# Additions, copies and word tiles of a fused attention and MoE kernel moved between ScalarE and VectorE, and matrix products moved ahead of the scores

## The chip, the cores and the metric

The kernel runs on one core of a Trainium2 chip. The time is that of the device in microseconds, from the core's start to its end, and the median of several runs counts. A core has a matrix engine (TensorE, PE in the rows), a vector engine (VectorE, DVE), an engine for functions and copies (ScalarE, ACT), GpSimd (POOL) for plain element work, and SyncE (SP), whose queue issues every DMA of this kernel. Each engine runs its own instructions in the order in which they were written; between engines only semaphores order the work.

## The reference

Four batches of eight heads of windowed attention, with 576 rows of 64 numbers per head, give the rows x (2304 by 512). Then follow two layers without a residual path:

```python
scores = where(mask, q @ k.T / 8, -1e9)             # plain window of 32 (heads 0-3) or dilated by 4 (heads 4-7)
p = exp(scores - max); attn = p / (p.sum(-1) + 1e-9) @ v
x = attn.transpose(0, 2, 1, 3).reshape(2304, 512)
h = x @ w_in                                        # layer one, w_in and w_out are 64-bit floats
x = (h - tanh(h)) @ w_out
logits = x @ phi                                    # layer two: 32 slots, 8 experts
d = softmax over rows; c = softmax over slots
out = c @ concat_e(relu((d.T @ x)_e @ w1[e]) @ w2[e])
```

The epsilon 1e-9 in the denominator of the attention, the copies that bring q and k into place, and the conversion of the 64-bit words of w_in and w_out are what the change touches.

## The kernel before, in words

The rows are taken in five chunks: the first 512 of each batch (chunks 0 to 3), and one last chunk of what is left over of all four. A chunk needs the attention of its batch (values split into a high part `xhi` and a low part `xlo`), and layer one: 16 tiles of h, each of 12 matmuls of 128 by 512 (high by high, low by high, high by low; `emit_h`, L559 to L561), a tanh on ScalarE (L565), a subtraction on VectorE (L568), a transposition on VectorE (L581) and small products with phi (`emit_logits`, L574).

The attention of batch 0 stands alone at the start (0 to about 62 us), written out by a list of due times. The attention of batch 1 is interleaved with layer one of chunk 0, two tiles of h a step in eight steps 0 to 7 (`mixed_step`); batches 2 and 3 are interleaved in the same way with chunks 1 and 2 (`phase_step`). An attention is cut into 12 units. A unit is: scores into one PSUM tile (L349, behind a product that lays down the mask, L331), a maximum over them on VectorE (L359), three or four exponentials with row sums on ScalarE (L362), the epsilon (L371) and a reciprocal (L373) on VectorE, the norm on GpSimd (L374), transposition by TensorE (L383) and a copy of it, and the products with v (L404), whose results go to `xhi` (ScalarE) and `xlo` (VectorE, L440). In batches 0 and 1 q and k are transposed by TensorE (L307) and copied by the engines that the table `ENGS['qk']` names, A for ScalarE and V for VectorE (L102 and L315 or L317).

Chunk 0 also converts the weights. A 64-bit word is turned into a float by a ScalarE instruction on the upper half (`conv_a`, L492) and two VectorE instructions that shift in bits of the lower half (`conv_b`, L500 and L501). For a w_in tile the high part is rounded by a copy (L513, shown under the helper's line L102, engine by `ENGS['wh']`), and the low part is a subtraction on GpSimd (L514). A w_out tile is stored to DRAM, and multiplied with phi at once (`conv_out_c`: transposition L522 and copy; `conv_out_d`: four products L533 and a copy; `conv_out_e`: L546).

The raw words are loaded by SP, two tiles a DMA (L467 w_in, L471 w_out), into places in `gt` that earlier raw words held. A DMA waits until those are read, and the ones behind it in the queue wait with it. A converted w_in tile lies in one place, `b[:, 3]` of `cvb`, until L514 has read it; w_out tiles have four places in `cva`. Of PSUM, the five tiles `mm` go round among all of this.

What each step issues in which order stands in `mixed_step`, L935 to L984.

Of the kernel before, what the change touches and what calls it, by code (L numbers as in the profile page):

```python
# [14 lines left out]
ALU = mybir.AluOpType  # L15
# [20 lines left out]
    ("out", 0): 0, ("out", 2): 1, ("out", 4): 2, ("in", 0): 3, ("in", 2): 0, ("in", 4): 1, ("out", 6): 2, ("in", 6): 3,  # L36
    ("out", 8): 2, ("out", 10): 1, ("in", 8): 2, ("in", 10): 3, ("out", 14): 2, ("in", 14): 3,
}
ENGS = {'qk': 'AAAAVAAVVVAA', 'pt': 'AAA', 'hi': 'AAA', 'rem': 'VVA', 'wh': 'V', 'wt': 'AV', 'wq': 'V', 'wp': 'A'}
WARM = 5  # L40
NWARM = 4
WAT = 0.29
# [21 lines left out]
def moe_kernel(ctx: ExitStack, tc: tile.TileContext, q, k, v, w_in, w_out, phi, w1, w2, out):  # L64
# [258 lines left out]
    def emit_scores(b, i):  # L323
        p, u = PO[i // 3], i % 3
        nb, nq, nk = shape(i)
        ps = mm([128, nb, nk])
        mask = mask_d[:, (0, 4, 2)[u]:(4, 8, 6)[u]] if nb == 4 else mask_p[:, min(u, 1):min(u, 1) + 3]
        by_pe = b < MASKPE
        nr = nq if by_pe else 64
        if by_pe:  # L330
            nc.tensor.matmul(  # L331
                ps.rearrange("p c k -> p (c k)"), lhsT=id2.rearrange("p a k -> p (a k)"),
                rhs=mask[0:64].rearrange("p c k -> p (c k)"), start=True, stop=True,
            )
        for c in range(nb):
            for x in range(2):
                step = 1
                if nb == 4:

                    r2, qi = divmod(2 * u + c // 2, 3)  # L340
                    q0 = 288 * (c % 2) + 144 * r2
                    q0, k0 = q0 + nq * qi, q0 + max(0, nq * qi - 32)
                    if b in VB:
                        q0, k0 = (288 * (c % 2) + r2 + 2 * (t - 288 * (c % 2) - 144 * r2) for t in (q0, k0))
                        step = 2
                else:
                    q0, k0 = nq * (nb * u + c), max(0, nq * (nb * u + c) - 32)
                r = slice(64 * x, 64 * x + 64)
                nc.tensor.matmul(  # L349
                    ps[64 * x:64 * x + nr, c, :], lhsT=qT[b, p][r, q0:q0 + step * (nr - 1) + 1:step],  # L350
                    rhs=kT[b, p][r, k0:k0 + step * (nk - 1) + 1:step],
                    start=not by_pe, stop=True, skip_group_check=True,
                )
        pr = prs.next()[:, 0:nb * nk].rearrange("p (c k) -> p c k", c=nb)
        if not by_pe:
            nc.vector.tensor_tensor(out=pr, in0=ps, in1=mask, op=ALU.add)
            ps = pr
        nm = tiny("nm", 4, 3)[:, 0:nb]
        nc.vector.tensor_reduce(out=nm, in_=ps, op=ALU.max, axis=AX.X, negate=True)  # L359
        sm = tiny("smm", 4, 3)[:, 0:nb]  # L360
        for c in range(nb):
            nc.scalar.activation(  # L362
                out=pr[:, c, :], in_=ps[:, c, :], func=ACTF.Exp, bias=nm[:, c:c + 1],
                accum_out=sm[:, c:c + 1],
            )
        sc_s[b, i] = (pr, sm)

    def emit_norm(b, i):
        nb, nq, nk = shape(i)
        pr, sm = sc_s.pop((b, i))  # L370
        nc.vector.tensor_scalar(out=sm, in0=sm, scalar1=EPS, scalar2=None, op0=ALU.add)  # L371
        rc = tiny("rc", 4, 3)[:, 0:nb]
        nc.vector.reciprocal(out=rc, in_=sm)  # L373
        nc.gpsimd.tensor_tensor(out=pr, in0=pr, in1=rc.unsqueeze(2).to_broadcast([128, nb, nk]), op=ALU.mult)  # L374
        sc_p[b, i] = pr
# [101 lines left out]

    def conv_tiles():
        a, b = unit("cva", [128, 4, 512]), unit("cvb", [128, 4, 512])
        convs["out"], convs["in"] = Ring([a[:, n] for n in range(4)]), Ring([b[:, 3]])  # L480
        convs["wt"] = Ring([b[:, 0].rearrange("p (a b) -> p a b", a=4), b[:, 1].rearrange("p (a b) -> p a b", a=4)])
        convs["wq"] = b[:, 2].rearrange("p (a b) -> p a b", a=4)

# [11 lines left out]
    def conv_b(kind, ft):  # L495
        wl, _ = raw_t.pop((kind, ft))
        f = cvt[kind, ft]
        du = f.bitcast(U32)
        dk = like(f, kind).bitcast(U32)
        nc.vector.tensor_scalar(out=du, in0=du, scalar1=3, scalar2=None, op0=ALU.logical_shift_left)  # L500
        nc.vector.scalar_tensor_tensor(  # L501
            out=dk, in0=wl, scalar=29, in1=dk, op0=ALU.logical_shift_right, op1=ALU.bitwise_or
        )
# [60 lines left out]
    def emit_tanh(ps, g):  # L564
        nc.scalar.activation(out=g, in_=ps, func=ACTF.Tanh)  # L565
# [308 lines left out]
    with tc.manual_schedule():  # L874
# [60 lines left out]
        def mixed_step(an, ch, s, xh, xl, gs, posts):  # L935

            a, b = 2 * s, 2 * s + 1
            if s == 0:
                an.load(3, 2)
            if s < 6:  # L940
                load_w("in", 4 + a)
            if s < 5:
                load_w("out", 6 + a)
            pa, gs[a] = emit_first(ch, xh, xl, a, first), gring.next()
            emit_tanh(pa, gs[a])
            emit_sub(pa, gs[a])
            if s < 7:
                conv_a("in", 2 + a)

            if s:  # L950
                for n in (a - 2, a - 1):
                    emit_gT(ch, n, gs[n])
            an.turn(s)
            if s < 7:
                conv_b("in", 2 + a)
                conv_in_c(2 + a)
            if 0 < s < 6:
                conv_out_c(4 + a)
                conv_out_c(5 + a)
            if s in (2, 4, 6):  # L960
                conv_out_e(3 + a)
            if s < 5:
                conv_a("out", 6 + a)
                conv_a("out", 7 + a)
                conv_b("out", 6 + a)
                conv_b("out", 7 + a)
            if s < 7:
                conv_a("in", 2 + b)
            pb, gs[b] = emit_first(ch, xh, xl, b, first), gring.next()
            emit_tanh(pb, gs[b])  # L970
            an.score(2 * s)
            emit_sub(pb, gs[b])
            an.score(2 * s + 1)
            if s < 7:
                conv_b("in", 2 + b)
                conv_in_c(2 + b)
            an.norms(s)
            an.values(s)
            if 0 < s < 6:
                conv_out_d(4 + a)  # L980
                conv_out_d(5 + a)
            if s:
                emit_logits(ch, a - 1, gs[a - 1])
            emit_logits(ch, a, gs[a])  # L984
# [38 lines left out]
        for ch in range(4):  # L1023
            xh, xl = xhi[ch], xlo[ch]
            if ch == 3:
                late.insert(0, sb.tile([128, 2048], F32, tag="qk", name="ex"))
                xr = unit("xr", [128, 2, KT, 256], F32R)
                nc.scalar.copy(out=xr[:, 0], in_=xrem)
                nc.vector.tensor_tensor(out=xr[:, 1], in0=xrem, in1=xr[:, 0].bitcast(F32), op=ALU.subtract)
                home(0, late)  # L1030
                load_experts()
                gring = Ring(glast)
            else:
                gring = gts
            gs, nxt = {}, None
            for s in range(NFT // 2):
                (phase_step if ch else mixed_step)(an, ch, s, xh, xl, gs, posts)
# [202 lines left out]
```

## Time and profile before

| | |
|---|---|
| median of 3 runs | 473.22 us (471.66 to 473.87) |
| the profiled execution | 473.43 us, of which the span from the first to the last instruction is 471.6 us |
| TensorE busy | 437.3 us, 93% of the span |
| VectorE | 262.3 us, 56% |
| ScalarE | 198.3 us, 42% |
| GpSimd | 77.0 us, 16% |

Matmuls are pipelined, so that TensorE's share is not one of its peak. The shares are means over stages that differ: up to 62 us the attention of batch 0 runs with filler matmuls, from 62 to 157.5 us chunk 0 with the weights' conversion, then three chunks, the rest, and the experts. In the timelines a row is one instruction or several like it: start, duration, engine, line, operation, tile written and tiles read, shapes, count, and in brackets the idle time of the engine before it and what ended that.

### The profile page before, as it was taken

The numbers are of one execution on the slowest core, as the hardware profiler recorded it, in microseconds if no ns is written. First come the engines' busy times: TensorE is split into PE (matmuls) and PEld (weight loads), VectorE is DVE, ScalarE is ACT, GpSimd is POOL, SyncE is SP. The second block draws the span as 40 slices with busy tenths as digits, with TensorE's granted clock in tenths as the row PEclk, the third lists the DMA queues.
The fourth block names the chain that finished last, engine by engine and source line by source line (L and its number), as shares of the span: only waits on it lengthen the run. The fifth ranks groups of instructions, "written<-read, shape, count | busy, mean of one in ns | idle before, by whom it ended". The sixth has DMA issues, their size and how long they took to land.

```text
span 471.6 us, 11459 instructions
## 1 busy us (share of the span) xinstructions
PE 437.3 (93%) x4615; PEld 318.6 (68%) x4615; DVE 262.3 (56%) x631; ACT 198.3 (42%) x683; POOL 77.0 (16%) x95
## 2 busy tenths in 40 slices
PE   6989897998999999999999999999999999999981
PEld 4766566875777685888776778776777689645330
DVE  1555569898887675666575786362744251232141
ACT  3777546664653163564244445422122222213131
POOL 3221313233133331213112031100000000010000
PEclk9999997998999999999999999999999999999996
DMA  8999934966465403162333120248000789899938
GB/s 245 226 238 317 280 146 135 258 179 231 131 169 108 94 1 51 41 89 39 81 67 54 37 41 3 90 182 355 0 1 5 265 318 403 348 375 408 409 131 329
DMA packets 88260, 81.15 MB, mean 172 GB/s; under 512 B 63888, under 2 KB 67728, under 8 KB 88208
## 3 DMA queue, kind: packets, MB, share of 16 engines
q1 hardware_dynamic: 88208, 80.43, 56.0%
q8 instruction: 36, 0.59, 0.5%
q14 instruction: 16, 0.13, 0.1%
HBM read 71.50 MB, written 8.91 MB: 170 GB/s over the span
## 4 chain that ended last, share of the span: by engine, by line
PE 60%; issue 12%; DVE 10%; ACT 7%; DMA 6%; POOL 1%; SPq 1%; ACTq 0%; DVEq 0%; POOLq 0%
PE h L559 11%; PE h L561 10%; PE h L560 10%; PE mm L349 4%; ACT mem L362 4%; PE lg L574 3%; PE h L782 3%; PE mm L404 3%; PE y L807 3%; PE mm L698 3%; PE mm L383 3%; DVE cva L501 2%; DMA raww<-in_moe_w_out_dram 2%; DMA v<-in_v_dram 1%; DMA rqk<-in_k_dram 1%
## 5 line engine op out<-in xcount | busy, mean ns | idle before, releaser
L559 PE MATMUL h<-xhi,wts 128*128 128x512 f32 x256 | 106.6, 416 | 1.1 <-DVE wts L102 0.7
L561 PE MATMUL h<-xhi,wts 128*128 128x512 f32 x256 | 101.3, 396 | 2.0 <-POOL wts L514 2.0
L560 PE MATMUL h<-xlo,wts 128*128 128x512 f32 x256 | 101.2, 395 | 0.0
L565 ACT ACTIVATE mem<-h 128x512 f32<-128x512 f32 x72 | 42.9, 596 | 135.1 <-PE h L561 127.7
L568 DVE TENSOR_TENSOR mem<-h,mem 128x512 f32<-128x512 f32 x72 | 49.4, 686 | 79.8 <-ACT mem L565 79.7
L559 PEld LDWEIGHTS h<-xhi,wts 128*128 128x128 f32 x256 | 49.0, 191 | 17.5 <-issue 5.8
L561 PEld LDWEIGHTS h<-xhi,wts 128*128 128x128 f32 x256 | 48.6, 190 | 14.5 <-POOL wts L514 3.7
L374 POOL TENSOR_TENSOR mem<-mem 128x320 f32<-128x320 f32 (+1 forms) x48 | 33.4, 704 | 148.4 <-DVE mem L373 79.8
L560 PEld LDWEIGHTS h<-xlo,wts 128*128 128x128 f32 x256 | 48.9, 191 | 8.9 <-DVE xlo L440 0.3
L581 DVE STREAM_TRANSPOSE gt<-mem 128x512 f32<-128x512 f32 x64 | 41.1, 684 | 0.0
L362 ACT ACTIVATE mem<-mem 128x80 f32<-128x80 f32 (+1 forms) x84 | 29.7, 355 | 15.6 <-DVE mem L359 15.6
L349 PE MATMUL mm<-qk 64*64 64x96 f32 (+2 forms) x672 | 34.2, 245 | 1.9 <-ACT qk L315 1.7
L362 ACT ACTIVATE mem<-mm,mem 128x80 f32<-128x80 f32 (+1 forms) x84 | 26.9, 338 | 17.4 <-DVE mem L359 17.2
L349 PEld LDWEIGHTS mm<-qk 64*64 64x64 f32 (+1 forms) x672 | 27.5, 132 | 8.6 <-ACT qk L315 3.3
L514 POOL TENSOR_TENSOR wts<-cvb,wts 128x512 fp32r<-128x512 f32 x16 | 20.6, 1289 | 73.6 <-DVE wts L102 34.9
L102 ACT COPY mem<-mm 96x384 f32<-96x384 f32 (+4 forms) x64 | 26.3, 439 | 8.6 <-PE mm L383 6.9
L383 PE MATMUL mm<-mem 112*80 112x112 f32 (+1 forms) x168 | 23.9, 276 | 5.0 <-ACT cvb L492 2.7
L574 PE MATMUL lg<-mem 128*32 128x128 f32 x576 | 25.9, 279 | 0.9 <-DVE mem L568 0.9
L404 PE MATMUL mm<-mem,v 80*64 80x48 f32 (+1 forms) x672 | 26.0, 226 | 0.5 <-ACT mem L102 0.5
L404 PEld LDWEIGHTS mm<-mem,v 80*64 80x64 f32 (+1 forms) x672 | 22.1, 137 | 5.4 <-issue 2.2
L383 PEld LDWEIGHTS mm<-mem 112*80 112x80 f32 (+1 forms) x168 | 16.7, 125 | 9.5 <-POOL mem L374 4.4
L574 PEld LDWEIGHTS lg<-mem 128*32 128x32 f32 x576 | 15.3, 109 | 11.3 <-issue 9.0
(170 smaller groups left out, 643.4 us busy)
## 6 DMA issues: line engine op xcount, KB each, us to landing
ex<-in_moe_w_dram SPq DMA_DIRECT2D x21, 1024.0 KB, 10.7
gt<-in_moe_w_out_dram SPq DMA_DIRECT2D x7, 1024.0 KB, 8.1
gt<-in_moe_w_in_dram SPq DMA_DIRECT2D x7, 1024.0 KB, 7.8
gt<-in_moe_w_dram SPq DMA_DIRECT2D x6, 1024.0 KB, 11.5
mem<-in_moe_w_dram SPq DMA_DIRECT2D x5, 1024.0 KB, 8.3
wo_dram<-cva SPq DMA_DIRECT2D x16, 256.0 KB, 6.2
wo<-wo_dram SPq DMA_DIRECT2D x4, 1024.0 KB, 7.9
out_dram<-o SPq DMA_DIRECT2D x8, 512.0 KB, 4.8
```

The source lines that it names most:

```text
L349: nc.tensor.matmul(ps[64 * x:64 * x + nr, c, :], lhsT=qT[b, p][r, q0:q0 + step * (nr - 1) + 1:step], rhs=kT[b, p][r, k0:k0 + step * (nk - ...
L362: nc.scalar.activation(out=pr[:, c, :], in_=ps[:, c, :], func=ACTF.Exp, bias=nm[:, c:c + 1], accum_out=sm[:, c:c + 1],)
L374: nc.gpsimd.tensor_tensor(out=pr, in0=pr, in1=rc.unsqueeze(2).to_broadcast([128, nb, nk]), op=ALU.mult)
L383: nc.tensor.transpose(ps[:, c, :], pr[0:P, c, :], ident[0:P, 0:P])
L404: nc.tensor.matmul(o[64 * hh:64 * hh + 64, col:col + nq], lhsT=vt[b, p](n, hh), rhs=pt[:, c, 64 * x:64 * x + nq], start=True, stop=True,)
L559: nc.tensor.matmul(ps, lhsT=wh, rhs=xh[:, kt, :], start=(n == 0), stop=False)
L560: nc.tensor.matmul(ps, lhsT=wh, rhs=xl[:, kt, :], start=False, stop=False)
L561: nc.tensor.matmul(ps, lhsT=wl, rhs=xh[:, kt, :], start=False, stop=(n == KT - 1))
L565: nc.scalar.activation(out=g, in_=ps, func=ACTF.Tanh)
L568: nc.vector.tensor_tensor(out=g, in0=ps, in1=g, op=ALU.subtract)
L574: nc.tensor.matmul(lgs[ch][32 * j:32 * j + 32, 0:128], lhsT=wp[:, ft, :], rhs=g[:, 128 * j:128 * j + 128], start=(ft == 0), stop=(ft == NF ...
L581: nc.vector.transpose(out=gt[:, ft, :], in_=g)
```

## The change

Six edits, of which the first reaches all four batches:

- The epsilon is added by a ScalarE instruction right behind a unit's exponentials (L366 in the changed kernel), not by VectorE in front of the reciprocal.
- In batch 1 all four copies of q and k of a pair are ScalarE's (two of them were VectorE's).
- The copy that rounds the high part of a w_in tile is ScalarE's for all 16 tiles.
- A converted w_in tile has a second place, `glast[4]`, in a region of `mem` that held g tiles; so chunk 0 has five places for g tiles instead of six, and chunk 1 begins elsewhere in the ring.
- In a step, the conversion of both w_in tiles stands earlier: the even tile's `conv_b` ahead of the transpositions L581, the odd tile's `conv_a` and `conv_b` before the second tile of h; the low part of the odd tile follows the second tanh.
- The products with phi (`conv_out_d`, L533) stand ahead of the scores, not behind the products with v.

```diff
-ENGS = {'qk': 'AAAAVAAVVVAA', 'pt': 'AAA', 'hi': 'AAA', 'rem': 'VVA', 'wh': 'V', 'wt': 'AV', 'wq': 'V', 'wp': 'A'}
+ENGS = {'qk': 'AAAAAAAAVVAA', 'pt': 'AAA', 'hi': 'AAA', 'rem': 'VVA', 'wh': 'A', 'wt': 'AV', 'wq': 'V', 'wp': 'A'}
...
                 accum_out=sm[:, c:c + 1],
             )
+        nc.scalar.activation(out=sm, in_=sm, func=ACTF.Copy, bias=EPS)
         sc_s[b, i] = (pr, sm)

     def emit_norm(b, i):
         nb, nq, nk = shape(i)
         pr, sm = sc_s.pop((b, i))
-        nc.vector.tensor_scalar(out=sm, in0=sm, scalar1=EPS, scalar2=None, op0=ALU.add)
...
-        convs["out"], convs["in"] = Ring([a[:, n] for n in range(4)]), Ring([b[:, 3]])
+        convs["out"], convs["in"] = Ring([a[:, n] for n in range(4)]), Ring([b[:, 3], glast[4]])
...
             if s < 7:
                 conv_a("in", 2 + a)
-
+                conv_b("in", 2 + a)
             if s:
                 for n in (a - 2, a - 1):
                     emit_gT(ch, n, gs[n])
             an.turn(s)
             if s < 7:
-                conv_b("in", 2 + a)
+                conv_a("in", 2 + b)
                 conv_in_c(2 + a)
+                conv_b("in", 2 + b)
...
-            if s < 7:
-                conv_a("in", 2 + b)
             pb, gs[b] = emit_first(ch, xh, xl, b, first), gring.next()
             emit_tanh(pb, gs[b])
+            if s < 7:
+                conv_in_c(2 + b)
+            if 0 < s < 6:
+                conv_out_d(4 + a)
+                conv_out_d(5 + a)
             an.score(2 * s)
             emit_sub(pb, gs[b])
             an.score(2 * s + 1)
-            if s < 7:
-                conv_b("in", 2 + b)
-                conv_in_c(2 + b)
             an.norms(s)
             an.values(s)
-            if 0 < s < 6:
-                conv_out_d(4 + a)
-                conv_out_d(5 + a)
...
-                gring = gts
+                gring = gts if ch else Ring([gts.places[n] for n in (0, 1, 2, 4, 3)])
+                gts.n += 4 * (ch == 1)
```

ScalarE's order in step 0, from the first tanh (L565) to the exponentials (L362), before. Here `cvb` is the even or odd w_in tile, `cva` a w_out tile:

```order
L565 ACTIVATE mem<-h 128x512
L492 ACTIVATE cvb<-gt 128x512
L102 COPY qk<-mm 128x3x2x48
L315 ACTIVATE qk<-mm 128x3x2x48
L492 ACTIVATE cva<-gt 128x512 x2
L492 ACTIVATE cvb<-gt 128x512
L565 ACTIVATE mem<-h 128x512
L362 ACTIVATE mem<-mm,mem 128x80 x8
```

The same stretch of ScalarE now, where L492 and the CAST with `mem` belong to the odd w_in tile in its second place, and L366 is the epsilon:

```order
L565 ACTIVATE mem<-h 128x512
L492 ACTIVATE cvb<-gt 128x512
L102 COPY qk<-mm 128x3x2x48 x2
L315 ACTIVATE qk<-mm 128x3x2x48 x2
L492 ACTIVATE mem<-gt 128x512
L102 CAST wts<-cvb 128x4x128
L492 ACTIVATE cva<-gt 128x512 x2
L565 ACTIVATE mem<-h 128x512
L102 CAST wts<-mem 128x4x128
L362 ACTIVATE mem<-mm,mem 128x80 x4
L366 ACTIVATE mem<-mem 128x4
L362 ACTIVATE mem<-mm,mem 128x80 x4
```

Two copies, two roundings and the two additions have come in, and the odd w_in tile now stands ahead of the two w_out tiles.

VectorE's order in the same step, from the even w_in tile's second instruction (L501 on `cvb`) to the reciprocals (L373), before:

```order
L501 SCALAR_TENSOR_TENSOR cvb<-gt,cvb 128x512
L102 CAST wts<-cvb 128x4x128
L500 TENSOR_SCALAR cva<-cva 128x512
L501 SCALAR_TENSOR_TENSOR cva<-gt,cva 128x512
L500 TENSOR_SCALAR cva<-cva 128x512
L501 SCALAR_TENSOR_TENSOR cva<-gt,cva 128x512
L359 TENSOR_REDUCE mem<-mm 128x4
L568 TENSOR_TENSOR mem<-h,mem 128x512
L359 TENSOR_REDUCE mem<-mm 128x4
L500 TENSOR_SCALAR cvb<-cvb 128x512
L501 SCALAR_TENSOR_TENSOR cvb<-gt,cvb 128x512
L102 CAST wts<-cvb 128x4x128
```

VectorE now, from the same instruction (`mem<-mem` and `mem<-gt,mem` of L500 and L501 are the odd w_in tile):

```order
L501 SCALAR_TENSOR_TENSOR cvb<-gt,cvb 128x512
L500 TENSOR_SCALAR mem<-mem 128x512
L501 SCALAR_TENSOR_TENSOR mem<-gt,mem 128x512
L500 TENSOR_SCALAR cva<-cva 128x512
L501 SCALAR_TENSOR_TENSOR cva<-gt,cva 128x512
L500 TENSOR_SCALAR cva<-cva 128x512
L501 SCALAR_TENSOR_TENSOR cva<-gt,cva 128x512
L359 TENSOR_REDUCE mem<-mm 128x4
L568 TENSOR_TENSOR mem<-h,mem 128x512
L359 TENSOR_REDUCE mem<-mm 128x4
L373 RECIPROCAL mem<-mem 128x4 x2
```

The odd w_in tile has moved from behind the two maxima to ahead of the w_out tiles, and so ahead of the maxima.

TensorE's order at the end of step 1, behind the second tile of h, before:

```order
L561 MATMUL h<-xhi,wts 128x512
L331 LDWEIGHTS mem
L331 MATMUL mm<-mem 128x320
L349 MATMUL mm<-qk 48x80 x8
L331 LDWEIGHTS mem
L331 MATMUL mm<-mem 128x320
L349 MATMUL mm<-qk 48x80 x8
L404 MATMUL mm<-mem,v 64x48 x16
L533 MATMUL mm<-cvb,mem 32x128 x8
L574 MATMUL lg<-mem 32x128 x8
```

The same stretch of TensorE now:

```order
L561 MATMUL h<-xhi,wts 128x512
L533 MATMUL mm<-cvb,mem 32x128 x8
L331 LDWEIGHTS mem
L331 MATMUL mm<-mem 128x320
L349 MATMUL mm<-qk 48x80 x8
L331 LDWEIGHTS mem
L331 MATMUL mm<-mem 128x320
L349 MATMUL mm<-qk 48x80 x8
L404 MATMUL mm<-mem,v 64x48 x16
L574 MATMUL lg<-mem 32x128 x8
```

The products L533 have moved ahead of both scores. The order of SP's DMAs is the same in both kernels.

## Rows read from the trace of the kernel before

**Rows 1.** Busy time in steps 1, 3, 4 of chunk 0; last columns clock, DMA share, GB/s.
```profile
67.12:85.96 18.84, 15.64 (x155) 12.45 (x151) 17.19 (x32) 12.22 (x45) 5.01 (x5) 0.82 0.42 128
...
100.17:114.88 14.71, 12.24 (x141) 9.50 (x137) 11.86 (x29) 8.21 (x29) 3.93 (x4) 0.99 0.74 251
114.88:129.65 14.77, 14.08 (x139) 11.10 (x135) 12.38 (x28) 7.88 (x27) 3.82 (x4) 0.90 0.50 139
```

**Rows 2.** Timeline of TensorE in step 1 and in chunk 1.
```profile
74.84 1.71 PE L383 MATMUL mm<-mem 112*80 112x112 f32 x8 [2.69 <-ACT cvb L492]
...
77.91 0.78 PE L559 MATMUL h<-xhi,wts 128*128 128x512 f32 x1
...
180.07 1.47 PE L698 MATMUL mm<-gt,mem 32*32 32x512 f32 x33 [0.67 <-DVE xlo L440]
```

**Rows 3.** Waits of TensorE from 60 to 165 us: total, times, longest.
```profile
PE mm L533 <- ACT mem L362: 3.2, 3, 2.3
...
PE h L561 <- POOL wts L514: 1.0, 2, 0.6
```

**Rows 4.** Timeline of ScalarE: conversions, copies, and small instructions.
```profile
54.78 0.66 ACT L492 ACTIVATE cvb<-gt 128x512 f32<-128x512 f32 x1 [1.24 <-POOL wts L514]
...
64.18 0.54 ACT L102 COPY qk<-mm 128x288 f32<-128x288 f32 x1
64.55 0.55 ACT L315 ACTIVATE qk<-mm 128x288 f32<-128x288 f32 x1
...
109.50 1.26 ACT L492 ACTIVATE cva<-raww 128x512 f32<-128x512 f32 x2 [3.26 <-DMA raww<-in_moe_w_out_dram]
...
193.40 0.19 ACT L362 ACTIVATION_READ_ACCUMULATOR mem<-mem 128x1 f32 x1
193.49 0.30 ACT L102 CAST xhi<-mm 128x96 fp32r<-128x96 f32 x2
193.69 0.21 ACT L102 COPY mem<-mm 128x64 f32<-128x64 f32 x1
193.79 0.32 ACT L102 CAST xhi<-mm 128x192 fp32r<-128x192 f32 x1
...
246.90 0.28 ACT L639 ACTIVATE mem<-mem 128x1 f32<-128x1 f32 x1
```

**Rows 5.** DMA issues on SP's queue at the start of step 3.
```profile
100.07 0.39 SPq L467 DMA_DIRECT2D gt<-in_moe_w_in_dram  x1
100.56 1.32 SPq L471 DMA_DIRECT2D raww<-in_moe_w_out_dram  x1
```

**Rows 6.** Timeline of VectorE in steps 0 to 2.
```profile
67.13 1.65 DVE L501 SCALAR_TENSOR_TENSOR cva<-gt,cva 128x512 uint32<-128x512 uint32 x1
...
69.76 0.48 DVE L359 TENSOR_REDUCE mem<-mm 128x4 f32<-128x320 f32 x1
...
72.33 0.43 DVE L102 CAST wts<-cvb 128x512 fp32r<-128x512 f32 x1
72.67 0.16 DVE L371 TENSOR_SCALAR mem<-mem 128x4 f32<-128x4 f32 x1
...
73.03 1.09 DVE L371 TENSOR_SCALAR mem<-mem 128x4 f32<-128x4 f32 x1
...
98.86 0.42 DVE L500 TENSOR_SCALAR cvb<-cvb 128x512 uint32<-128x512 uint32 x1
99.31 0.69 DVE L501 SCALAR_TENSOR_TENSOR cvb<-gt,cvb 128x512 uint32<-128x512 uint32 x1
```

**Rows 7.** Timeline of GpSimd in steps 0 and 1.
```profile
66.84 1.39 POOL L514 TENSOR_TENSOR wts<-cvb,wts 128x512 fp32r<-128x512 f32 x1 [8.12 <-DVE wts L102]
...
72.84 1.26 POOL L514 TENSOR_TENSOR wts<-cvb,wts 128x512 fp32r<-128x512 f32 x1 [4.61 <-DVE mem L371]
```

**Rows 8.** Pieces of the chain that ended last, batch 0: start, us, what.
```profile
20.86 0.09 DVE mem L371
...
23.15 1.35 ACT mem L362 x8
```

## The prediction

> **What bounds the kernel now.** I read the engines' shares first (TensorE 93%, so only its idle and slow stretches can be won), then the windows by step, the waits of TensorE, and the timelines around those waits, last the chain and SP's queue. The reader is to see three things.
>
> First, chunk 0 is where TensorE loses time. Step 1 takes 18.84 us and step 4 14.77 with the granted clock at 0.82 and 0.90; step 3 takes 14.71 with TensorE busy for 12.24 of it [rows 1]. [...] In step 3 the second product with phi L533 waits 2.3 us for the exponentials of the step's first scores, whose PSUM tile it takes; three such waits make 3.2 us [rows 3].
>
> Second, what feeds the stall of step 3 is a DMA: ScalarE stood 3.26 us at the w_out words (109.50) with tanh and exponentials queued behind [rows 4]. That DMA was issued at 100.56, right behind the w_in one at 100.07 [rows 5], which waited for the place that the odd w_in tile's L501 of step 2 read last, from 99.31 to 100.00 [rows 6].
>
> Third, VectorE is held by GpSimd. An L501 that takes 0.69 took 1.65 from 67.13, a second L371 1.09 from 73.03 where the one ahead took 0.16 [rows 6]; both end just behind an L514 of GpSimd (66.84 + 1.39, 72.84 + 1.26) [rows 7].
>
> **The change part by part.** The sum is made against the profiled execution, 473.43 us, of which 471.60 are span; that is 0.2 above the median of the runs.
>
> Epsilon on ScalarE, batch 0. No row shows an ACTIVATE of 128x4 that waits for the accumulator read in front of it. Without a wait a small copy costs 0.10 (193.69 to 193.79), which is the low end. [...] High end: 0.19 of read and all 0.28 of the 128x1 ACTIVATE, 0.47 [rows 4]. I take 0.26, nearest to the copy. The chain of batch 0 goes through eleven units' exponentials and from ten of them on through ScalarE's next work (at 23.15, say, eight instructions of 1.35 us that chain on to a copy) [rows 8], so 10 x 0.26 = 2.6 come in. L371 lies on that chain six times, each time 0.26 from the instruction before it to the reciprocal (0.09 of it shown); at one of them the scores behind ScalarE's copies would be later anyway, so 5 x 0.26 = 1.3 go. Net +1.3; with the bounds -0.3 to +3.4.
>
> Second place for a word tile. The odd tile's L492 at 54.78 waited 1.24 for GpSimd [rows 4]. Now it waits for ScalarE's own queue: the even tile's rounding, two copies to xhi and two others, 1.45 us from the end of L501 at 52.94, so it starts at 54.4. Of 1.24 only 0.4 go: -0.4 (0 to -1.2).
>
> Steps 0 and 1. Four copies of q and k stand on ScalarE instead of two. They are 0.37 apart (64.18, 64.55) [rows 4], so the first scores start up to 2 x 0.37 later, and TensorE has nothing else: +0.4 after 0.3 that VectorE's own copies took longer. Behind the copies come the odd L492 (to 66.4), the even rounding (0.66 like the L492, to 67.0), and GpSimd's L514 from 67.0 to 68.3. VectorE does the odd pair from 66.4 to 67.5 (1.1 from 0.42 and 0.69 [rows 6]), is then held to 68.3, does a w_out pair to 69.4, is held again by the odd tile's L514 (69.2 to 70.5), and comes to the first maximum at 71.6, where before it was 69.76 [rows 6]. Then nothing of the conversion is left behind the maxima, so exponentials and norms run through: two times 1.35 and 0.26, reciprocal, norm, and the second transpositions end at about 76.5. Before, they ended at 74.84 + 1.71 [rows 2]. So the stall and its slow clock stay, and this term is +0.4 (-3.5 to +1.5, the ends under the rivals).
>
> [...]
>
> L533 ahead of the scores. Its two tiles now come from copies that were read long before, not from exponentials: -3.2 [rows 3]. The products need the two copies of L522's results; the VectorE one ends about 6 us behind the step's first tanh, when the second tile of h is just done. Cover gone, that is a wait of some tenths. With the idle stretch of step 3 the low clock of step 4 goes: 0.10 of 14.77 lost is 2.95 us at the half level [rows 1], work for 1.5: -1.5. The DMA wait of 3.26 goes too: the odd pair of step 2 is done some 6 us earlier, and so are both DMAs [rows 5]; the place of those words was last read by TensorE in step 1.
>
> Low parts earlier. The h matmuls L561 that waited for L514, 1.0 in two [rows 3]: the later one (0.6) goes, -0.6.
>
> What is late next, steps 2 to 4. VectorE has, from a step's tanh to its first maximum, a subtraction, four pairs of 1.1, two transpositions and three copies, some 7.2 us, and up to two holds by GpSimd of 1.3; then ScalarE two units of exponentials and epsilon, 2.5, and xhi, 0.55. That is 10.2 to 12.8, where TensorE alone needs 12.3 in step 3 (14.71 - 2.34, less some tenths of others) [rows 1]. I take +0.5 for the three steps (0 to +2).
>
> The roundings moved. One is 0.43 on VectorE (72.33) and like an L492, 0.66, on ScalarE [rows 4, 6]; from step 1 on each is covered by the 2.7 us of h behind it, and costs nothing; with that cover gone, 0.66. [...]
>
> Chunks 1 and 2. L698 waits 0.67 for the low parts, which stand behind ScalarE's exponentials, two copies and a tanh (180.07; the same wait in chunk 2) [rows 2]. Two epsilons are 0.52 more, 0.24 of it slack between copy and tanh: +0.28 each, +0.55. Elsewhere there TensorE waits for nothing.
>
> Sum: 1.3 - 0.4 + 0.4 - 3.2 - 1.5 - 0.6 + 0.5 + 0.55 = -2.95, so 470.5 us. What the runs can tell from no change is about 0.5%, 2.4 us; 470.5 lies just beyond that.
>
> **The rivals.**
>
> B, VectorE isn't held twice in step 0. If the odd tile's L514 comes behind the second w_out pair, the first maximum is 1.1 earlier, the idleness in step 1 falls below what cost the clock, and the 0.82 of step 1 goes. Of 18.84, 0.18 is 6.8 us at half clock, less 2.1 that fell into idleness: work for 2.4 [rows 1]. 470.5 - 1.1 - 2.4 = 467.0. For it: starts differ by a tenth in my walk. Against it: each L514 is now released by ScalarE in the middle of VectorE's pairs.
>
> C, slower: ScalarE becomes the engine that others wait for. Place: the epsilon behind each unit, batch 0 first. At 0.47 instead of 0.26, 18 of them on the path (ten in batch 0, four in chunks 1 and 2, four in steps 2 to 4) add 3.8; with step 1 and 2 ending later by 1.5 and 0.9, as a hold in front of the maximum then meets a late ScalarE, 470.5 + 6.2 = 476.7. It decides from 0.42 a piece on. For it: batch 0's chain is ScalarE's. Against it: the 0.10 of the small copy.
>
> D, the early DMA isn't early: another wait in SP's queue keeps the w_out words late. Then the 2.3 and 1.5 of steps 3 and 4 stay: 474.3. Against it: nothing else stood between 100.07 and 100.56.
>
> **How the numbers follow.** Forecast 0.42, with 469 to 472 as its own range; B 0.25; C 0.17; D 0.06; the rest, 0.10, has no case. Faster by over 0.5%: half of the forecast, B, 0.04 of the rest: 0.50. Slower: C and 0.03: 0.20. Within: 0.30. The range of 8 in 10 reaches over B's and most of C's bounds: 466.5 to 476.
>
> **What would show it.** In the profile after: L366's distance to the next ScalarE instruction (0.26), and the end of batch 0 about 1 us later; a wait at L383 in step 1 with a low clock behind it; no wait of L492 for a DMA in step 3, and the clock at 1.00 in step 4; no L533 that waits for L362; L500 or L501 held over 1 us beside an L514, twice a step; L698 waiting about 0.95. Step 1 without its stall, or a batch 0 longer by 3 us, would make the prediction wrong.

## The result, and the profile after

The changed kernel takes 474.64 us in the median of 20 runs against 472.12 for the kernel before: a ratio of 1.0057, 95% interval 1.0037 to 1.0077. It is slower by half a per cent, where 470.5 and faster was forecast. Three of the 20 runs took 480.7 to 482.1 us at a granted clock of 0.952 to 0.964, where the others have 0.979 to 0.986, and the ratio leaves out two of them. The profiled execution of it took 474.69 us with a span of 472.70.

The windows by step, with the columns of [rows 1]; here are steps 1, 3, 4 and 5 of the changed kernel.

```profile
68.71:89.22 20.51, 16.12 (x151) 12.51 (x151) 15.35 (x27) 13.65 (x48) 7.33 (x6) 0.83 0.40 121
...
103.60:117.21 13.61, 12.33 (x137) 9.52 (x137) 10.86 (x23) 9.50 (x31) 4.46 (x4) 1.00 0.74 257
117.21:130.19 12.98, 12.72 (x135) 10.08 (x135) 10.22 (x24) 10.32 (x36) 4.72 (x4) 1.00 0.56 173
130.19:142.85 12.66, 11.20 (x121) 8.61 (x121) 8.57 (x21) 8.26 (x31) 3.98 (x5) 1.00 0.55 100
```

Step 3 is 1.1 us shorter than in [rows 1] and step 4 is 1.8 shorter with the clock at 1.00, but step 1 is 1.7 longer, and TensorE still idles for 1.28 of step 3's 13.61. The waits of TensorE in chunk 0 (from 62 to 165 us, as this kernel comes to chunk 0 later) tell why; they answer to [rows 3].

```profile
PE mm L383 <- ACT qk L102: 1.7, 2, 1.2
PE mm L307 <- ACT mem L362: 1.6, 1, 1.6
PE mm L533 <- DVE cvb L102: 1.5, 1, 1.5
PE mm L404 <- DVE cvb L102: 1.1, 1, 1.1
PE mm L383 <- ACT mem L362: 1.1, 1, 1.1
PE mm L349 <- ACT qk L315: 0.5, 1, 0.5
PE h L561 <- POOL wts L514: 0.5, 1, 0.5
```

The 3.2 us of L533 behind the exponentials are gone. L404 and another L533 now wait for copies on VectorE, 2.6 in two. Step 1's wait of 2.69 [rows 2] has become three, 3.9 in all.

A second trace of the kernel before (the first experiment) is needed to lay the times side by side. That execution took 471.37 us, 2.1 less than the one that the forecast was summed against. TensorE comes to the second group of L307 at 11.92 us in it, where the first trace has 13.13. In the first trace the warming matmuls and the scores around 8 to 12 us are slow for longer (a group of sixteen L349 takes 1.30 at 10.70 there, 0.76 at 10.13 in the second), though the granted clock reads 1.00 from 0 to 12 us in both. From that L307 to the end of step 0 both take the same. All lengths in us, a step's end being the end of its last L574 and the last row ending where the last L574 starts:

| stretch | before, first trace | before, second | changed | changed less second |
|---|---|---|---|---|
| start to second group of L307 | 13.13 | 11.92 | 11.81 | -0.1 |
| to the end of step 0 | 54.06 | 54.07 | 56.90 | +2.8 |
| step 1 | 18.84 | 18.01 | 20.51 | +2.5 |
| step 2 | 14.21 | 14.21 | 14.38 | +0.2 |
| step 3 | 14.70 | 15.13 | 13.61 | -1.5 |
| step 4 | 14.78 | 14.23 | 12.98 | -1.3 |
| steps 5 to 7, end of chunk 0 | 31.22 | 31.19 | 30.89 | -0.3 |
| end of chunk 0 to the last L574 | 244.43 | 244.49 | 245.37 | +0.9 |

Steps 3 and 4 are 2.8 us shorter. Batch 0 with step 0, step 1, and chunks 1 and 2 take 6.2 more. Of steps 5 to 7, step 5 is 1.2 longer (12.66 against 11.47), and steps 6 and 7 are 1.5 shorter. Step 1 isn't the same in each execution of one kernel (18.84 and 18.01 before), so up to 1 us of its difference can be chance.

**Epsilon.** ScalarE of the changed kernel behind a unit's exponentials:

```profile
15.71 0.20 ACT L362 ACTIVATION_READ_ACCUMULATOR mem<-mm,mem 128x1 f32 x1
15.94 0.20 ACT L366 ACTIVATE mem<-mem 128x4 f32<-128x4 f32 x1
16.05 0.93 ACT L315 ACTIVATE qk<-mm 128x288 f32<-128x288 f32 x2
```

From the read to what follows L366 it is 0.34, where 0.09 stood before (193.40 to 193.49 in [rows 4]): 0.25 a unit, as forecast (0.26).

**Step 1.** VectorE and GpSimd in step 0, then TensorE.

```profile
67.98 0.69 DVE L501 SCALAR_TENSOR_TENSOR mem<-gt,mem 128x512 uint32<-128x512 uint32 x1
68.60 1.49 DVE L500 TENSOR_SCALAR cva<-cva 128x512 uint32<-128x512 uint32 x1
...
70.73 1.52 DVE L500 TENSOR_SCALAR cva<-cva 128x512 uint32<-128x512 uint32 x1
...
72.90 0.48 DVE L359 TENSOR_REDUCE mem<-mm 128x4 f32<-128x320 f32 x1
```

```profile
68.07 1.74 POOL L514 TENSOR_TENSOR wts<-cvb,wts 128x512 fp32r<-128x512 f32 x1 [8.25 <-ACT wts L102]
70.21 1.76 POOL L514 TENSOR_TENSOR wts<-mem,wts 128x512 fp32r<-128x512 f32 x1 [0.40 <-ACT wts L102]
```

```profile
74.82 0.47 PE L307 MATMUL mm<-mem,rqk 96*128 96x96 f32 x3 [1.63 <-ACT mem L362]
76.38 0.55 PE L383 MATMUL mm<-mem 112*80 112x112 f32 x4 [1.10 <-ACT mem L362]
78.10 0.94 PE L383 MATMUL mm<-mem 112*80 112x112 f32 x4 [1.16 <-ACT qk L102]
...
80.39 0.78 PE L559 MATMUL h<-xhi,wts 128*128 128x512 f32 x1
```

Both L500 of w_out start under an L514 and end 0.28 behind its end (68.07 + 1.74 = 69.81, 70.21 + 1.76 = 71.97). The first maximum comes at 72.90, 3.1 later than in [rows 6], or 4.5 later counted from the second group of L307. The exponentials and with them L307 and both groups of L383 are late, and the h matmuls behind start at the lower level, nine of them up to 84.3. The lower level is a granted clock of 0.50 here (78 to 84 us) and most of the h matmuls take 0.63 at it; the upper one is 1.00, where most take 0.39.

### The profile page after: what moved, and what is told of

Same layout as the page of the kernel before. It is cut to its first block, busy times and chain, and to the rows that moved or that the text cites. A ratio compares the mean times of both kernels' runs of the same rounds, so it can differ in the third digit from the quotient of the medians.

```text
span 472.7 us, 11386 instructions
## 1 busy us (share of the span) xinstructions
PE 436.5 (92%) x4615; PEld 318.3 (67%) x4615; DVE 243.1 (51%) x559; ACT 218.4 (46%) x755; POOL 81.1 (17%) x95
## 4 chain that ended last, share of the span: by engine, by line
PE 64%; issue 12%; ACT 11%; DVE 8%; DMA 2%; POOL 1%; SPq 0%; ACTq 0%; POOLq 0%
PE h L559 11%; PE h L561 10%; PE h L560 10%; PE mm L349 5%; ACT mem L362 4%; PE lg L574 4%; PE mm L404 3%; PE h L782 3%; PE y L807 3%; PE mm L698 3%; PE mm L383 3%; DVE cva L500 1%; ACT qk L102 1%; DVE cva L501 1%; PE warm L204 1%
## 5 line engine op out<-in xcount | busy, mean ns | idle before, releaser
L561 PE MATMUL h<-xhi,wts 128*128 128x512 f32 x256 | 101.0, 394 | 1.3 <-POOL wts L514 1.3
L565 ACT ACTIVATE mem<-h 128x512 f32<-128x512 f32 x72 | 43.0, 598 | 126.9 <-PE h L561 119.5
L374 POOL TENSOR_TENSOR mem<-mem 128x320 f32<-128x320 f32 (+1 forms) x48 | 33.7, 704 | 169.2 <-DVE mem L373 155.6
L561 PEld LDWEIGHTS h<-xhi,wts 128*128 128x128 f32 x256 | 48.5, 189 | 13.2 <-POOL wts L514 2.6
L581 DVE STREAM_TRANSPOSE gt<-mem 128x512 f32<-128x512 f32 x64 | 41.1, 684 | 0.0
L362 ACT ACTIVATE mem<-mm,mem 128x80 f32<-128x80 f32 (+1 forms) x84 | 26.8, 330 | 22.5 <-DVE mem L359 22.4
L362 ACT ACTIVATE mem<-mem 128x80 f32<-128x80 f32 (+1 forms) x84 | 29.7, 355 | 15.8 <-DVE mem L359 15.8
L349 PE MATMUL mm<-qk 64*64 64x96 f32 (+2 forms) x672 | 33.9, 244 | 3.3 <-ACT qk L315 3.3
L349 PEld LDWEIGHTS mm<-qk 64*64 64x64 f32 (+1 forms) x672 | 27.2, 131 | 10.3 <-ACT qk L315 4.6
L404 PE MATMUL mm<-mem,v 80*64 80x48 f32 (+1 forms) x672 | 26.6, 228 | 1.9 <-DVE cvb L102 1.4
L383 PE MATMUL mm<-mem 112*80 112x112 f32 (+1 forms) x168 | 23.5, 272 | 4.5 <-ACT qk L102 1.7
L404 PEld LDWEIGHTS mm<-mem,v 80*64 80x64 f32 (+1 forms) x672 | 22.5, 139 | 7.2 <-issue 2.2
L574 PE MATMUL lg<-mem 128*32 128x128 f32 x576 | 25.9, 279 | 0.9 <-DVE mem L568 0.9
L574 PEld LDWEIGHTS lg<-mem 128*32 128x32 f32 x576 | 14.9, 109 | 11.6 <-issue 9.0
L383 PEld LDWEIGHTS mm<-mem 112*80 112x80 f32 (+1 forms) x168 | 16.5, 123 | 8.8 <-POOL mem L374 3.8
L373 DVE RECIPROCAL mem<-mem 128x4 f32<-128x4 f32 (+1 forms) x48 | 7.9, 168 | 27.3 <-ACT mem L366 27.3
```

What stands on the lines that cost most here:

```text
L349: nc.tensor.matmul(ps[64 * x:64 * x + nr, c, :], lhsT=qT[b, p][r, q0:q0 + step * (nr - 1) + 1:step], rhs=kT[b, p][r, k0:k0 + step * (nk - ...
L362: nc.scalar.activation(out=pr[:, c, :], in_=ps[:, c, :], func=ACTF.Exp, bias=nm[:, c:c + 1], accum_out=sm[:, c:c + 1],)
L383: nc.tensor.transpose(ps[:, c, :], pr[0:P, c, :], ident[0:P, 0:P])
L404: nc.tensor.matmul(o[64 * hh:64 * hh + 64, col:col + nq], lhsT=vt[b, p](n, hh), rhs=pt[:, c, 64 * x:64 * x + nq], start=True, stop=True,)
L561: nc.tensor.matmul(ps, lhsT=wl, rhs=xh[:, kt, :], start=False, stop=(n == KT - 1))
L574: nc.tensor.matmul(lgs[ch][32 * j:32 * j + 32, 0:128], lhsT=wp[:, ft, :], rhs=g[:, 128 * j:128 * j + 128], start=(ft == 0), stop=(ft == NF ...
```

## Experiments

All ran beside the kernel before; medians of it there were 471.7 to 471.9. Ratios are to the kernel before, with 95% intervals. A difference of two medians from different experiments is less certain than that of the two ratios, and the two can differ by some tenths.

**The kernel before again.**

> The kernel before, unchanged. The profiled execution of it took 473.43 us, its twenty timed runs have a median of 472.12. Theory R: the profile showed an execution above the typical one, because one of its slow clock stretches (step 1 or step 4 of chunk 0) isn't there in every execution; then the granted clock over the run varies between runs with their time (about 0.98 at 473.5, 0.985 or more at 471), and a second profile may show step 4 at 1.00 and some 13.3 us instead of 14.77. Then the 1.5 us that the prediction took for the clock of step 4 was worth less to begin with. Rival: the clock is the same in all of them and the 1.3 us lie elsewhere (DMA at the start); step 4 is 14.8 again.

Median 471.34, ratio 0.9998 (0.9977 to 1.0019). Its trace has step 4 at 0.94 and 14.23 us, not at 1.00. Most of the difference to the first trace lies in neither step but at the start (1.2 us, above), with 0.8 in step 1, whose clock is 0.91 where it was 0.82. Theory R holds in kind: the executions of one kernel differ in where the clock is low (step 3 is at 0.95 here, 0.99 in the first trace), and the one profiled first stood at the upper end. The place was another than expected.

**Epsilon alone on the kernel before.**

```diff
+        nc.scalar.activation(out=sm, in_=sm, func=ACTF.Copy, bias=EPS)
...
-        nc.vector.tensor_scalar(out=sm, in0=sm, scalar1=EPS, scalar2=None, op0=ALU.add)
```

> The kernel before with epsilon added on ScalarE (L366) in place of VectorE's L371, nothing else. Theory E (epsilon is most of what the whole change loses): +1.3 us in batch 0, +0.9 in the two L698 waits, and some tenths in steps 1 to 7, so 474.5 to 475 against 472.1. Theory C (the order of the conversions in steps 0 and 1 is most of it): batch 0's +1.3 is partly taken back at the wait for the weights of h(0) and in step 1's idleness, whose second L371 was held 1.1 us by GpSimd before and no longer exists: 472.5 to 473.5.

Median 477.09, ratio 1.0104 (1.0072 to 1.0136): worse than either theory, whose upper end, 475, lies just outside the interval. In its trace, batch 0 from that L307 to the end of step 0 takes 55.39, so +1.33; chunks 1 and 2 take 1.2 more. Step 1 is as before (18.1). The L533 of step 3 now waits 2.96 instead of 2.34, and step 4 takes 15.5.

**Only L533 in front of the scores.**

```diff
+            if 0 < s < 6:
+                conv_out_d(4 + a)
+                conv_out_d(5 + a)
             an.score(2 * s)
```

> The kernel before with the products with phi (L533) put in front of the step's scores, nothing else. The forecast priced this at -3.2 us of waits. The w_out words still come late, as the w_in place isn't doubled here, so ScalarE's 3.26 us at the DMA in step 3 stay and the second L533, now earlier in TensorE's order, waits for the copies behind it. If the tile's PSUM place alone was the cause: 469 to 470. If the late words were the cause: the 2.3 us become a wait of L533 for VectorE's or ScalarE's copy, and the time is 471.5 to 473.

Median 471.09, ratio 0.9980 (0.9961 to 0.9999), between the two theories. This is the term that the forecast put at -3.2 and, with the clock, at -4.7. TensorE of the kernel before in step 3, then ScalarE, VectorE and TensorE of this kernel:

```profile
113.96 0.43 PE L533 MATMUL mm<-cvb,mem 128*32 128x128 f32 x8 [2.34 <-ACT mem L362]
```

```profile
108.40 1.24 ACT L492 ACTIVATE cva<-raww 128x512 f32<-128x512 f32 x2 [3.51 <-DMA raww<-in_moe_w_out_dram]
```

```profile
110.63 0.69 DVE L501 SCALAR_TENSOR_TENSOR cva<-raww,cva 128x512 uint32<-128x512 uint32 x1
111.24 0.48 DVE L102 COPY cvb<-mm 128x128 f32<-128x128 f32 x2
111.64 0.45 DVE L359 TENSOR_REDUCE mem<-mm 128x3 f32<-128x288 f32 x1
```

```profile
106.99 0.64 PE L533 MATMUL mm<-cvb,mem 128*32 128x128 f32 x16
...
111.58 0.67 PE L404 MATMUL mm<-mem,v 80*64 80x48 f32 x16 [1.61 <-DVE cvb L102]
```

L533 itself no longer waits. But the tile that it fills is read by a copy on VectorE, which stands behind the two w_out pairs (late, for the words were), and L404 of the second unit takes that same PSUM tile. The wait moved one place on along the tiles, from 2.34 at L533 to 1.61 at L404.

**The whole change with epsilon left on VectorE.** The edit is the second one in reverse, on the changed kernel.

> The changed kernel with epsilon back on VectorE (L371), all else of the change kept. Theory E: without the 1.5 us that batch 0 grew and the 1.0 of chunks 1 and 2, 471 to 472, so no slower than the kernel before. Theory C: L371 behind GpSimd's L514 or L374 is held again by 1.1 us in each step of chunk 0 and the maxima of step 1 stay late, so 473 to 474, little below the changed kernel's 474.6.

Median 470.72, ratio 0.9988 (0.9969 to 1.0008). Epsilon is worth 3.9 us of the changed kernel by the medians and 3.3 by the ratios, and all the rest of the change comes to -1.0 or -0.6, not told from nothing. Theory E stands; of Theory C's price for L371 nothing is seen. Of the 48 L371 of this kernel the longest takes 0.69; the median is 0.17, and the two of step 1 up to 76 us take 0.17 each. The hold has gone over to the L500 of w_out (1.49 at 66.47 and 1.53 at 68.59), and step 1 takes 18.77:

```profile
66.57:85.34 18.77, 14.87 (x151) 11.40 (x151) 15.86 (x30) 13.26 (x47) 7.35 (x6) 0.91 0.36 106
```

**Epsilon by batches.**

```diff
+        if b in (0,):
+            nc.scalar.activation(out=sm, in_=sm, func=ACTF.Copy, bias=EPS)
...
+        if b not in (0,):
             nc.vector.tensor_scalar(out=sm, in0=sm, scalar1=EPS, scalar2=None, op0=ALU.add)
```

> The kernel before with epsilon on ScalarE in batch 0 alone (the units ahead of the first chunk); batches 1 to 3 keep VectorE's L371. All of epsilon cost 5.4 us in the kernel before (477.1 against 471.7), of which its trace shows 1.3 at the end of batch 0 and 1.2 in chunks 1 and 2. Theory A (only the chain grows): +1.3, so 473.0. Theory B (the longer waits of TensorE in batch 0 also let its clock fall, as in the changed kernel's trace from 30.3 to 33.2 us, where TensorE's work took twice as long): +2.5 to +3.5 in the median, 474 to 475, and a spread of the runs above 2 us.

Median 474.29, ratio 1.0043 (1.0025 to 1.0061), 2.4 above 471.89. In its trace batch 0 grew by 1.36 and kept its clock (1.00 up to 50 us); step 3's wait of L533 was 2.90 and step 4 took 15.3, ten of its matmuls at the lower level (from 115.84 on, most of them 0.63). So Theory B's amount came, in this trace at another place than batch 0. In the three traces with VectorE's epsilon in batches 0 and 1 (both of the kernel before, and the next run) that wait is 1.95 to 2.34; why it grows with epsilon is open.

> The kernel before with epsilon on ScalarE in batches 2 and 3 alone, which chunks 1 and 2 carry. The forecast put +0.28 on each of the two L698 waits, +0.55 in all; the trace of all epsilons on ScalarE shows +1.2 from the end of chunk 0 to the last L574, as L698 waits there a second time, for ScalarE's copy L662. Expected by the trace: 472.6 to 473.0 against 471.7. By the forecast's term: 472.2.

Median 473.49, ratio 1.0038 (1.0018 to 1.0058). The trace gives +0.9 in chunks 1 and 2 (245.36 to the last L574); the interval holds that and not the forecast's 0.55.

> The changed kernel (474.6) with epsilon back on VectorE in batch 0 alone; batches 1 to 3 keep it on ScalarE. With all of epsilon back on VectorE it was 470.7, 3.9 less. Theory B (batch 0: 1.3 us of chain and a stretch at the lower clock behind it): 472 or a little under, with no stretch below 0.9 of the clock between 29 and 50 us. Rival (chunk 0's steps 1 to 7 and chunks 1 and 2 carry it): 473.3, only the chain's 1.3 less, with the low stretch of batch 0 still there.

Here the changed kernel has epsilon on VectorE for batch 0 and on ScalarE behind it. Median 472.87, 1.8 below the changed kernel; ratio to before 1.0025 (0.9999 to 1.0052). Batch 0 is at 1.00 of the clock, as Theory B has it, but the time lies between the two sides. Step 1 of it:

```profile
66.14:86.66 20.52, 16.14 (x152) 12.49 (x151) 15.34 (x27) 13.67 (x48) 7.31 (x6) 0.83 0.39 123
```

The median is still 2.15 above the version with all of epsilon on VectorE. The two traces differ by 1.1: step 1 (20.52 against 18.77) and chunks 1 and 2 (1.0) are longer, step 4 is 1.6 shorter. Where the other 1.0 of the medians lies, the traces don't show.

**The changed kernel again.**

> The changed kernel, unchanged, for a second trace. Its first one had a stretch at the lower clock in batch 0, from 30.3 to 33.2 us behind a 1.27 us wait of TensorE for the copies of k, which cost 1.6 us. If that stretch comes with this kernel, it is there again. If it is chance, batch 0 ends 1.3 us behind that of the kernel before and the execution takes 473 to 473.5.

This one execution took 478.64. The window from 28 to 50 us of it and, in the second fence, of the first trace of the changed kernel:

```profile
28.00:50.00 22.00, 20.07 (x201) 14.05 (x202) 9.64 (x31) 14.62 (x54) 2.81 (x5) 0.69 0.89 237
```

```profile
28.00:50.00 22.00, 19.13 (x242) 13.81 (x241) 11.56 (x34) 15.14 (x61) 3.62 (x5) 0.92 1.01 282
```

```profile
29.35 1.02 PE L349 MATMUL mm<-qk 64*64 64x96 f32 x12 [1.27 <-ACT qk L315]
30.30 1.11 PE L522 MATMUL mm<-mem,cva 128*128 128x128 f32 x4
31.21 1.06 PE L204 MATMUL warm<-mem 128*128 128x256 bf16 x4
```

The low stretch is there again behind the same 1.27 us wait, and lasts to 44 us (0.50 from 32 on) instead of 33 (0.50 from 30 on in the first trace). In this trace step 1 takes 19.47 and step 4 13.00, against 20.51 and 12.98 in the first. In the third fence, of the first trace, four warming L204 take 1.06, which take 0.61 at the upper level later in that trace (34.90, a clock of 1.00). Where the wait is 1.03 (kernel before, both traces) the clock stays at 1.00 here. But the two kernels with epsilon added to the one before also wait 1.27 and 1.28 there and stay at 1.00 in their traces. The longer wait goes with the low stretch and doesn't bring it each time; what decides it stayed open.

**L533's copies on ScalarE.**

```diff
-... 'wq': 'V', ...
+... 'wq': 'A', ...
```

This diff is against the changed kernel with epsilon on VectorE; the three that follow are against this one.

> The changed kernel with epsilon on VectorE (470.7) and, besides, the copies of L533's products on ScalarE instead of VectorE. Theory Q: VectorE's queue holds these copies behind the two pairs L500/L501 of w_out, and L404 of the second unit waits for the PSUM tile that the first of them reads (1.14 us in step 3, and some of the clock behind it). Then L404's wait in step 3 goes and the time is 469 to 470. Rival: ScalarE's queue gives it back (the copies stand in front of the exponentials), or L404 then waits for the exponentials: 470.5 to 471.5.

Median 469.38, ratio 0.9936 (0.9913 to 0.9958). Theory Q stands: L404's wait in step 3 is gone.

```profile
100.77:113.04 12.27, 12.14 (x138) 9.44 (x137) 9.46 (x19) 8.29 (x24) 4.47 (x4) 1.00 0.87 314
```

Step 3 takes 12.27 with TensorE busy for 12.14, and step 4 13.04 at 1.00. It was the copy's place in VectorE's queue that made L404 wait. The wait of the second L533 in step 5 stays (1.47): that one is for its operand, VectorE's copy of L522's products, which this edit doesn't touch.

**The w_out pairs of step 0 behind the maxima.**

```diff
-                conv_b("out", 6 + a)
-                conv_b("out", 7 + a)
+                if s: conv_b("out", 6 + a), conv_b("out", 7 + a)
...
             an.score(2 * s + 1)
+            if s == 0:
+                conv_b("out", 6 + a)
+                conv_b("out", 7 + a)
```

> The kernel with epsilon on VectorE and L533's copies on ScalarE (469.4), and in step 0 the two pairs L500/L501 of w_out behind the second maximum instead of in front of the first. Leaves all work in. Theory H: in step 0 VectorE's two pairs are held by both L514 (1.48 and 1.52 us where one takes 0.42), so the first maximum comes at 71.8, and the exponentials, L307 and L383 of step 1 wait for it, 3.4 us in three waits, and lose the clock behind them. With the pairs behind, the first maximum comes at about 67.8, the waits go, and step 1 takes 15 to 16 us where it took 18.8: 466 to 467.5. Rival: the hold falls on the maxima (beside the L514 at 66.9), and the pairs now stand in front of the norms; step 1 keeps 2 us of waits and its low clock: 469 to 470.

Median 465.34, ratio 0.9856 (0.9821 to 0.9892), the best of all: 6.5 us under the kernel before, and a little better than Theory H has it. GpSimd, VectorE and TensorE of it, and step 1:

```profile
66.18 1.75 POOL L514 TENSOR_TENSOR wts<-cvb,wts 128x512 fp32r<-128x512 f32 x1 [8.22 <-ACT wts L102]
```

```profile
66.70 0.49 DVE L359 TENSOR_REDUCE mem<-mm 128x4 f32<-128x320 f32 x1
...
68.76 1.12 DVE L500 TENSOR_SCALAR cva<-cva 128x512 uint32<-128x512 uint32 x1
```

```profile
72.97 0.58 PE L383 MATMUL mm<-mem 112*80 112x112 f32 x4 [1.43 <-POOL mem L374]
73.91 0.58 PE L383 MATMUL mm<-mem 112*80 112x112 f32 x4 [0.35 <-POOL mem L374]
...
75.12 0.47 PE L559 MATMUL h<-xhi,wts 128*128 128x512 f32 x1
```

```profile
66.82:82.16 15.34, 13.06 (x152) 10.03 (x151) 13.18 (x26) 13.11 (x45) 7.53 (x6) 1.00 0.39 110
```

Counted from the second group of L307 (12.51 here, 13.27 in the version without the edit, whose first maximum starts at 71.78) the first maximum comes 4.3 us earlier. L307 waits no more, the waits of step 1 that are left are 1.8, and h starts at the upper level (0.47). Step 1 takes 15.34, at 1.00 of the clock. The hold is still there (1.12 for this L500, and 1.09 for an L501 at 73.31, beside L374), where nobody waits for it. The rival had it fall on the maxima, and it doesn't: the first one starts in the middle of an L514 (66.18 + 1.75 = 67.93) and takes 0.49. It reads a PSUM tile, where the L500 that are held (1.12 here) read SBUF alone.

**Two that gave nothing.**

```diff
-... 'wt': 'AV', ...
+... 'wt': 'AA', ...
```

> The kernel with epsilon on VectorE and L533's copies on ScalarE (469.4), and both copies of L522's products on ScalarE instead of one on each engine. Theory: in step 5 the second L533 waits 1.47 us for VectorE's copy, which stands behind an odd w_in pair (L500 held to 1.17, L501 0.69); on ScalarE, idle there from 136.6, it is 0.5 behind the first. So -1.4 from step 5: 468. Rival: in steps 1 to 4 ScalarE's copy stands in front of its L492 and delays VectorE's pairs by 0.5 each step, and the time stays at 469.4.

Median 469.32, ratio 0.9945 (0.9929 to 0.9961), as without. Step 5 did lose its wait (10.98 for 12.64). Batch 0 has these copies too, and there L404 now waits 0.32 and 0.80 for them: 1.4 us more by the end of step 0. Step 1 is 1.0 longer too (19.79 against 18.80).

```diff
-ENGS = {'qk': 'AAAAAAAAVVAA', ...
+ENGS = {'qk': 'AAAAVAAVVVAA', ...
```

> The kernel with epsilon on VectorE and L533's copies on ScalarE (469.4), with the q and k copies of batch 1 spread over ScalarE and VectorE as in the kernel before. The forecast has the four copies in one queue cost 0.4 in step 0 (L349 waits 0.52 for the second of k there). Expected by it: no wait of L349 in step 0 and step 0 shorter by 0.4, but VectorE has two copies of 0.4 more in front of its pairs, so the first maximum of step 1 comes no earlier: 469 to 469.4. Rival: with ScalarE freed, the roundings and so both L514 come earlier, the hold of VectorE ends earlier and step 1 shortens by 1: 468.

Median 469.76, ratio 0.9941 (0.9916 to 0.9967). The interval (467.8 to 470.2) holds both sides. Against the forecast, L349 waits 1.06 in step 0 for VectorE's copy, more than the 0.52 for ScalarE's. The rival had step 1 right, which shrinks by 0.9 (17.88), but step 3 takes back 1.2, as L533 there waits for VectorE again.

## Why the prediction was wrong, point by point

**Where the miss lies.** The forecast charged epsilon 1.3 and 0.55, and had the other five edits bring 4.8. Taken apart by the fourth experiment, epsilon cost 3.3 to 3.9, and the others brought 0.6 to 1.0. So the larger part of the miss is on the side of the gains, and most of those were to come from L533.

**L533 ahead of the scores: the step that failed.** "Its two tiles now come from copies that were read long before, not from exponentials: -3.2", and "a wait of some tenths" for the copies of L522. Alone, the edit brought 0.6 by the medians (471.09 against 471.68), 0.9 by the ratio, and 1.8 at the end of its interval. The prediction asked whose reader L533 waits for and not who waits for L533's reader. The same PSUM places go round: L404 waits 1.61 in step 3 of that kernel and 1.14 in the changed one, for a copy on VectorE behind w_out pairs. With the copies of L533's products moved to ScalarE's queue the forecast gain of step 3 came in full (12.27, where 14.71 less 2.34 was forecast). The "wait of some tenths" was mis-sized too. In step 5 of the changed kernel the second L533 waits 1.46 for VectorE's copy of L522's products, which stands behind the odd w_in pair, whose L500 is held:

```profile
136.71 1.17 DVE L500 TENSOR_SCALAR mem<-mem 128x512 uint32<-128x512 uint32 x1
137.91 0.69 DVE L501 SCALAR_TENSOR_TENSOR mem<-raww,mem 128x512 uint32<-128x512 uint32 x1
138.52 0.68 DVE L102 COPY cvb<-mm 128x512 f32<-128x512 f32 x1
```

```profile
139.26 0.42 PE L533 MATMUL mm<-cvb,mem 128*32 128x128 f32 x8 [1.46 <-DVE cvb L102]
```

With that copy on ScalarE the wait was gone (10.98 against 12.64 for step 5).

**Clock of step 4, -1.5.** The changed kernel's trace has it: 12.98 at 1.00. Two kernels with much the same wait in step 3 (1.61, and 1.14 with epsilon on VectorE) have step 4 at 0.88, 14.4 and 14.6 us. The gain was counted as if the stall were gone. With a wait of over 1 us left, the low stretch was there in two kernels and not in the changed one (13.0 at 1.00 in both of its traces, and with epsilon on VectorE in batch 0 alone); what decides it stayed open.

**Epsilon in batch 0, +1.3.** Right as a chain: 1.33 and 1.36 by the end of step 0. The 0.26 a unit was the author's estimate, and no row or run shows how it is made up; what the changed kernel's trace shows in its place is 0.25. In the median epsilon in batch 0 cost 1.8 to 2.4. What came on top wasn't a chain: the clock in the two traces of the changed kernel (the first loses some 1.7 there: 56.90 against 53.85 with epsilon on VectorE, less the chain's 1.35), and step 3's wait of L533 in the kernel before.

**Second place for a word tile, -0.4; low parts earlier, -0.6.** With epsilon on VectorE, the odd tile's L492 starts 0.6 earlier (41.07 us behind the second group of L307 for 41.65). The wait of L349 for the fourth copy (0.52) takes most of that back, and step 0 ends 0.2 earlier (53.85 for 54.06). The later L561 wait is gone and the earlier stays, as forecast.

**Steps 0 and 1, +0.4.** The mechanism was right: both holds, and the first maximum at 71.6 plus the 1.1 by which the first tanh came later, so 72.7, against 72.90. The hold left L371 and fell on the next conversion work of VectorE, L500 (1.49 and 1.52, above). The end was too early. The second transpositions end at 79.0 where 77.6 follows from the forecast, for L383's second tile is freed by the copies of q and k, which stand on ScalarE behind two units, two epsilons, a tanh and an L492. Without epsilon step 1 is 18.8, with it 20.5, 1.7 more for two additions, most of it in clock (0.91 and 0.83). The walk had exponentials and norms "run through", and so priced the additions on the exponentials' chain and not for the copies queued behind. In the second trace of the changed kernel step 1 is 19.47 at 0.82, so how much of the 1.7 belongs to the copies isn't settled. The roundings, charged at nothing, weren't run alone.

**Steps 2 to 4, +0.5; L698, +0.55.** Step 2 grew by 0.2; what came late next came in step 5 (above). In each of chunks 1 and 2 L698 now waits twice, the first time for ScalarE's copy L662. Chunk 1, then chunk 2:

```profile
178.98 1.05 PE L698 MATMUL mm<-gt,mem 32*32 32x512 f32 x6 [0.45 <-ACT mem L662]
...
180.47 4.41 PE L698 MATMUL mm<-gt,mem 32*32 32x512 f32 x122 [0.43 <-DVE xlo L440]
...
255.38 1.05 PE L698 MATMUL mm<-gt,mem 32*32 32x512 f32 x6 [0.78 <-ACT mem L662]
256.87 4.41 PE L698 MATMUL mm<-gt,mem 32*32 32x512 f32 x122 [0.44 <-DVE xlo L440]
```

In chunk 1 that is 0.88 in two where 0.67 stood, near the forecast +0.28. In chunk 2 it is 1.22 where 0.61 stood, and there lies what the term missed of the 0.9.

**The rivals.** B named the mechanism that was worth the most, the holds in front of the first maximum. VectorE was held twice, against B, and putting the held pairs behind the maxima brought 4 us. C had the sign and the engine right and the price wrong: epsilon costs 0.25, not the 0.42 from which it was to decide. D's words came earlier in the changed kernel (ScalarE has no DMA wait in step 3).

**The base.** The forecast was summed against an execution of 473.43, where the kernel's median is 472.1, so the forecast time started 1.3 too high. The gain of 2.95 from 472.1 would have been 469.2. The change moved the time by +2.5, so that the miss is 5.5 as a change and only 4.1 between the two times.

## What to carry to other kernels

When a matmul is moved to escape the reader of its PSUM tile, follow the tile two places on: who reads what the matmul writes, behind what in that engine's queue, and who fills the tile next. A small addition put on a busy engine delays each copy queued behind it (0.25 a unit here), not only its own chain. Look first at which instruction off the chain can go behind the one that others wait for: moving the two pairs here was worth 4 us, as much as taking epsilon back. Take a second trace of the kernel before where a forecast is below one per cent, since two profiled executions of the same kernel were 2.1 us apart here.

## What the runs showed of the hardware

- The hold went both ways. GpSimd's L514 took 1.27 where it began in the last 0.14 of an L501 (113.43 in the changed kernel, the L501 from 112.88 for 0.69) and 1.74 and 1.76 where an L501 had begun 0.09 before it (67.98 ahead of 68.07). The L500 behind that L501 was then held for the rest of the longer L514. So a pair that met an L514 in its L501 cost 0.5 on GpSimd, and 1.1 on VectorE where an L500 came next (1.49 and 1.52, where one takes 0.42 at 65.46).
- Not every VectorE instruction was held. Under an L514 the maximum L359 (0.49, from 66.70 in the version with the pairs behind the maxima) and the copy from PSUM that follows an L501 in step 1 of the changed kernel (0.68, from 81.60, the L514 from 81.08 for 1.76) keep their length, where L500, L501 and L371 were held by up to 1.1. Both of the first two read PSUM tiles.
- TensorE's granted clock differed in the same place of the same program: in batch 0 of the changed kernel it was 0.50 for 3 us in one trace (30 to 33) and for some 13 in another (up to 44).
- The matmuls of one program also differed in time where the granted clock reads 1.00 (0 to 12 us): at the start of the kernel before sixteen L349 took 0.76 from 10.13 in one trace and 1.30 from 10.70 in the other, which came to the next group of L307 1.2 us later. What decides it, the traces don't show.
